# Hedgehog linear attention beside a Mish feed-forward on one core: the kv sum in four column groups, and a new order of all steps

## The chip, the core and the metric

The kernel runs on one core of one Trainium2 chip. Five engines work side by side: TensorE (matmuls; PE in the profile, PEld for its weight loads), VectorE (DVE), ScalarE (ACT), GpSimd (POOL) and SyncE (SP), which here only issues DMA transfers. Each engine runs its own instructions in the order in which the program hands them to it, and semaphores tie the engines together. The metric is the device time of one execution in microseconds, lower is better; the median of several runs is given.

## The reference, cut to what matters

The input x has 2048 tokens of 448 features. It is normalized (LayerNorm without weights), goes through a linear attention of 16 heads of 28 features and, in parallel, through a feed-forward layer with Mish; both are added to x.

```python
xn = layernorm(x)                                    # [2048, 448]
# A: linear attention, H = 16 heads, Dh = 28
q, k, v = split_heads(xn @ wqkv)
pq, pk = einsum("bhsd,hdf->bhsf", q, w_phi), einsum("bhsd,hdf->bhsf", k, w_phi)
phi_q = concat([softmax(pq), softmax(-pq)], -1)      # 56 per head
phi_k = concat([softmax(pk), softmax(-pk)], -1)
kv = einsum("bhsf,bhsd->bhfd", phi_k, v)             # 56 x 28 per head
z  = einsum("bhsf->bhf", phi_k)
num = einsum("bhqf,bhfd->bhqd", phi_q, kv)
den = einsum("bhqf,bhf->bhq", phi_q, z)[..., None] + 1e-6
A = (num / den) merged over heads @ wo
# B: feed-forward, 1792 wide
h = xn @ w1 + b1
B = (h * tanh(softplus(h))) @ w2
out = x + A + B
```

## The kernel before

Tokens are worked on in 16 tiles of 128, taken in 8 pairs `u`. The program is a list of named steps, `ORDER` (L147). `run_order` calls them one after the other, and each call appends its instructions to the engines' streams; `Program.resolve` then puts in the waits that the data need. So `ORDER` alone sets the order on every engine and in every queue, and a step can put instructions on several engines at once. An engine does not pass over an instruction that waits.

The steps, in the names that the order uses (`u` is a pair, `t` a tile; a last letter names the engine: `d` DVE, `a` ACT, `p` POOL, `m` DMA, `s` SP's queue, `b` ACT and DVE with one half each):

- Loads. `lx0` to `lx6`: tiles of x (two tiles each; `lx4` and `lx6` four). `lkm`, `lkt`, `lvm`: the columns of wqkv for k, its last 64 rows for k and v, the columns for v, into `Wkv`. `lqT0` to `lqT3`: the q columns through a transposing DMA into `WqT` (`load_qT`, L285). `l1m0` to `l1m2`, `l1t`: W1. `l2`: the whole of W2 (`load_w2`, L305, one transfer). `lo`: Wo. `lp`, `lb`: w_phi and b1.
- `z16`: 16 matmuls on constants that keep TensorE busy while the first loads arrive.
- `pm`, `pw`, `pp`, `pk`, `pi`, `pv`: constants that POOL writes (masks, zeros, the identity, ones beside v). `pk` makes a second mask, `mask2`, and clears `KVT`.
- `st`, `rs`, `xn`, `xt`: statistics of one tile, reciprocal standard deviation of a pair, the normalized pair `xn`, and its transposed form `xnT`, through a DMA (`m`) or through TensorE. With `xn..p` the product runs on POOL and needs a small DVE instruction, `sh` (L489).
- `wtk`, `wmk`, `wmq`, `qd`: the weights of k and q are multiplied by w_phi (`Wbd`, made by `bd`), so that q and k are never formed. For k, `Wk` is transposed on TensorE and copied to `WT`; for q, `WqT` comes by DMA, and `qd` copies the last rows a second time on DVE (L289) once all four transfers are there.
- `v`, `k`, `q` with `u` and part 1 or 2: matmuls of one pair (8 in part 1, 6 in part 2; 64 rows each, two row halves of the array at a time). Part 2 is followed by the evacuation: v is copied to `v_all`, k and q go through two exponentials on ACT.
- `kn`: normalizes phi(k): a DVE sum and reciprocal, a POOL product (L635). `e`: a transposing DMA of phi(q) of one tile.
- `f0`, `f1`: the first feed-forward product for half of the tokens, then Mish on ACT.
- `kv` with `u` (L641): the sum of phi(k) times v over the pair's tokens. All pairs accumulate in one bank. The weights of a matmul are two heads of `v_all` with two more columns each (a one in each head's part, for z): 60 columns, placed in column group 0 or 64 of the array, so that two run side by side. What is streamed is phi(k) of the same two heads, 112 columns. Of the 60 x 112 products the blocks of one head with itself are wanted.
- `kvz` (L660): two DVE instructions of 60 partitions by 448 add an epsilon to the rows of z (`epsT`, made by `ep`) and multiply by `mask2`, which clears the blocks of one head with the other; then a transposing DMA makes `KVZ` from `KVT`.
- `nd` (L718): numerator and denominator of one tile, 16 matmuls of 56 rows, then seven or so DVE instructions to the quotient. `ot`: its transposed form.
- `G`, `g`, `wo`: the second feed-forward product and the output projection, into one bank per tile. `sto`, `stt`: stores.

PSUM has 8 banks; most matmul steps take two, the one least recently used.

Of the kernel before, what the change touches and what calls it, by code (L numbers as in the profile page):

```python
# [6 lines left out]
ALU = mybir.AluOpType  # L7
# [7 lines left out]
DH = 28  # L15
# [136 lines left out]
k51 xn0p v42a xt6m kn7.0 e2 k52 v52a kn1.1 xt0m kn7.1 kn5.0 v61a lbs q41 v62d kn4.0 k61 q42 e5 e6 l1ts v01d kn2.1 k62  # L152
# [16 lines left out]
def _kernel(es, nc, A_x, A_wqkv, A_w_phi, A_wo, B_w1, B_b1, B_w2, out):  # L169
# [10 lines left out]
    mask2 = sb("mask2", [P, 2, DH], FP32)  # L180
# [163 lines left out]
    def p_pads():  # L344
        for i in (1, 2, 0):
            op("POOL", lambda e, i=i: e.memset(Eq_of(i).rearrange("p i s (h n) -> p (i s h) n", n=64)[:, :, QP:64], 0.0),
               w=[("Eqp", i)] + ([(n, h) for n in ("WT", "WU") for h in range(2)] if i == 0 else []), tag=f"pp{i}")

    def p_mask2():
        op("POOL", lambda e: e.memset(mask2[:], 1.0), w=[("mask2",)], tag="pk0")  # L350
        for r in range(2):
            lo, hi = HALF[r]
            op("POOL", lambda e, lo=lo, hi=hi: e.affine_select(
                out=mask2[lo:hi], in_=mask2[lo:hi], compare_op=ALU.is_ge, fill=0.0, base=0, channel_multiplier=1,
                pattern=[[-(DH + 2), 2], [0, DH]]), r=[("mask2",)], w=[("mask2",)], tag="pk1")
            op("POOL", lambda e, lo=lo, hi=hi: e.affine_select(
                out=mask2[lo:hi], in_=mask2[lo:hi], compare_op=ALU.is_ge, fill=0.0, base=DH + 1, channel_multiplier=-1,
                pattern=[[DH + 2, 2], [0, DH]]), r=[("mask2",)], w=[("mask2",)], tag="pk2")
        op("POOL", lambda e: e.memset(KVT[:, :, :, :, :].rearrange("p g s x f -> p (g s x f)").bitcast(mybir.dt.uint32),
                                      0), r=[("mask2",)], w=[("KVT", 0), ("KVT", 1)], tag="pk3")  # L360

    def eps_rows():
        for i in range(2):
            op("DVE", lambda e, i=i: e.tensor_reduce(epsT[:, i:i + 1], ap_on(ident[:, DH + i:DH + i + 1],
                                                                          [[64, 2], [DH + 2, 2]]), AX.XY, ALU.add),
# [152 lines left out]
    def xT(u, eng):  # L518
# [6 lines left out]
        if eng == "both":  # L525
# [4 lines left out]
                 [("xnT", u)], f"xTe{u}")  # L530
# [110 lines left out]
    def kv_mm(u):  # L641
# [6 lines left out]
        def f(e):  # L648
            for par in range(2):
                for g in range(G):  # L650
                    for r in range(2):
                        ins = e.matmul(bank(kvb)[64 * r:64 * r + NDW, g * 2 * QP:(g + 1) * 2 * QP],  # L652
                                       v_all[:, u, par, 8 * r + 2 * g:8 * r + 2 * g + 2, :],
                                       E_of(u)[:, :, par, (4 * r + g) * QP:(4 * r + g + 1) * QP],
# [5 lines left out]
    def kvz():  # L660
        kvb = kv_bank[0]
        for r in range(2):
            lo, hi = 64 * r, 64 * r + NDW
            op("DVE", lambda e, r=r, lo=lo, hi=hi: e.scalar_tensor_tensor(
                ap_on(KVT[lo:hi, 0, 0, r, 0:1], [[P, 2 * G], [1, QP]]),
                ap_on(bank(kvb)[lo:hi, 0:1], [[QP, 2 * G], [1, QP]]), epsT[lo:hi, 2:3],
                ap_on(mask2[lo:hi, 0, 0:1], [[0, 2 * G], [1, QP]]), ALU.add, ALU.mult),
               r=[pb(kvb), ("mask2",), ("epsT", 2)], w=[("KVT", r)], tag=f"kvz{r}")
# [49 lines left out]
    def nd(t):  # L718
        b = take2(False)

        def f(e):
            for s in range(2):
                for g in range(G):
                    for r in range(2):
                        at = (s * G + g) * NDW
                        ins = e.matmul(bank(b + r)[:, at:at + NDW], EqT[64 * r:64 * r + QP, t, s * G + g, :],  # L726
                                       KVZ[64 * r:64 * r + QP, 2 * g + s, 64 * r:64 * r + NDW], start=True, stop=True)
# [224 lines left out]
    for n, fn in (("pi", p_ident), ("pm", p_mask), ("pw", p_wbd), ("pv", p_ones), ("pk", p_mask2), ("pp", p_pads)):  # L952
        add(n, fn)
# [55 lines left out]
```

## Time and profile before

| | us |
|---|---|
| median of three runs | 154.15 (153.95 to 154.91) |
| the profiled execution's own time | 154.01 |
| its span, first to last instruction | 152.1 |
| TensorE busy in the span | 145.4 |
| VectorE busy | 102.4 |
| ScalarE busy | 74.1 |
| GpSimd busy | 41.4 |

The profile shows one execution. Its page gives busy shares by engine and by forty slices of the span, the chain of work that ended last, and groups of like instructions with their mean duration and the idle time before them. Asked further, the trace gives the instructions of a stretch in order of time, the issues of SP's queue, and the busy time of every engine in chosen stretches. A row of the timeline reads: start, length from the first to the last of the group, engine (SPq is SP's issuing), line, operation, what is written from what, shape, how many, and in brackets the idle time of the engine before it and what ended it. A busy TensorE is not a TensorE at its peak, since a matmul's tail overlaps the next one. Line L438 holds the matmuls of v, k, q and f; L866 those of G and wo.

### The profile page before, as it was taken

Reading aid. Unit: us, or ns where it says so; the run is one execution under the profiler, and the core shown is the slowest. Engines: PE = TensorE matmul, PEld = TensorE weight load, DVE = VectorE, ACT = ScalarE, POOL = GpSimd, SP = SyncE. Lnnn points to the kernel's source line nnn. Section 1 sums busy time; section 2 is a strip of 40 time slices with the busy share of each in tenths; the row PEclk is TensorE's granted clock in tenths of the full one; section 3 lists DMA queues with packets and bytes.
Section 4 is the critical chain, followed back from the end, with each engine's and each line's share of the span. In section 5 each row is a group of like instructions: output and inputs, shape, how many; then the busy total and the mean of one; then the engine's idle time right before and its main releaser. Section 6 shows DMA issues by size and latency. Waiting matters only on the chain.

```text
span 152.1 us, 4002 instructions
## 1 busy us (share of the span) xinstructions
PE 145.4 (96%) x1735; PEld 76.1 (50%) x1735; DVE 102.4 (67%) x224; ACT 74.1 (49%) x96; POOL 41.4 (27%) x59
## 2 busy tenths in 40 slices
PE   7799997999899999999989999999999999999993
PEld 3475543556455584445434445444555555554552
DVE  0997999999999503059998378999373377252452
ACT  3889989796979994776756387100000000000000
POOL 7704743799899970000000000000000000000000
PEclk9999999999999999999999999999999999999999
DMA  5999759989999998840913510803300016003025
GB/s 136 294 136 337 156 166 161 251 158 136 198 190 173 251 271 207 157 89 0 98 37 59 39 26 0 65 2 65 60 0 4 16 49 181 0 4 60 0 100 201
DMA packets 39997, 17.24 MB, mean 113 GB/s; under 512 B 33964, under 2 KB 39212, under 8 KB 39980
## 3 DMA queue, kind: packets, MB, share of 16 engines
q1 hardware_dynamic: 39372, 16.87, 53.5%
q8 instruction: 13, 0.21, 0.6%
q10 hardware_dynamic: 608, 0.12, 0.4%
q14 instruction: 4, 0.03, 0.1%
HBM read 7.02 MB, written 1.84 MB: 58 GB/s over the span
## 4 chain that ended last, share of the span: by engine, by line
PE 69%; DVE 18%; SPq 6%; DMA 3%; ACT 2%; issue 1%
PE PS L438 32%; PE PS L866 28%; DVE stats L467 4%; PE PS L828 3%; SPq L285 3%; DMA x_all<-in_A_x_dram 3%; DVE v_all L745 3%; DVE v_all L747 2%; PE PS L652 2%; PE PS L726 2%; DVE v_all L749 2%; DVE xn L752 2%; DVE v_all L516 1%; DVE mv L468 1%; ACT actT L684 1%
## 5 line engine op out<-in xcount | busy, mean ns | idle before, releaser
L438 PE MATMUL PS<-xnT,W 64*128 64x512 bf16 x392 | 44.9, 376 | 0.9 <-ACT actT L623 0.5
L866 PE MATMUL PS<-W,actT 64*128 64x448 bf16 x392 | 38.7, 349 | 0.0
L703 ACT ACTIVATE actT<-PS,b1T 128x1024 bf16<-128x1024 f32 x28 | 29.8, 1113 | 13.4 <-PE PS L438 13.3
L438 PEld LDWEIGHTS PS<-xnT,W 64*128 64x128 bf16 x392 | 18.9, 94 | 21.7 <-DVE v_all L747 0.9
L866 PEld LDWEIGHTS PS<-W,actT 64*128 64x128 bf16 x392 | 18.8, 94 | 17.2
L635 POOL TENSOR_TENSOR actT<-actT,rSk 128x896 bf16<-128x896 bf16 x16 | 26.6, 1702 | 1.9 <-DVE rSk L633 1.3
L793 DVE TENSOR_TENSOR x_all<-PS,x_all 128x448 bf16<-128x448 f32 (+1 forms) x16 | 9.1, 615 | 15.8 <-PE PS L866 15.1
L631 DVE TENSOR_REDUCE Sk<-actT 128x32 f32<-128x896 bf16 x16 | 16.8, 1047 | 0.2
L741 DVE COPY Sq<-PS 128x16 f32<-128x16 f32 x32 | 4.0, 167 | 17.1 <-PE PS L726 17.0
L623 ACT ACTIVATE actT<-PS 128x896 bf16<-128x896 f32 x16 | 13.7, 923 | 1.0 <-PE PS L438 0.9
L438 PE MATMUL PS<-Wpk,xnT 64*128 64x448 bf16 x112 | 12.9, 350 | 1.0 <-DVE rSk L633 0.8
L438 PE MATMUL PS<-Wkv,xnT 64*128 64x448 bf16 x112 | 12.6, 349 | 0.0
L438 PE MATMUL PS<-Wpq,xnT 64*128 64x448 bf16 x112 | 12.5, 349 | 0.0
L467 DVE BATCH_NORM_STATS2 stats<-x_all 128x6 f32<-128x448 bf16 x14 | 8.5, 607 | 4.3 <-DMA x_all<-in_A_x_dram 4.3
L749 DVE TENSOR_TENSOR v_all<-v_all 128x464 f32<-128x464 f32 x16 | 10.3, 642 | 0.6
L745 DVE TENSOR_TENSOR v_all<-PS,Sq 128x464 f32<-128x464 f32 x16 | 10.3, 641 | 0.5
L752 DVE TENSOR_TENSOR xn<-v_all,rden 128x448 bf16<-128x448 f32 x16 | 10.0, 625 | 0.6
L747 DVE TENSOR_TENSOR v_all<-PS,Sq 128x464 f32<-128x464 f32 x16 | 10.1, 630 | 0.0
L684 ACT ACTIVATE actT<-PS 128x896 bf16<-128x896 f32 x10 | 8.6, 912 | 1.4 <-PE PS L438 1.4
L438 PEld LDWEIGHTS PS<-Wpk,xnT 64*128 64x128 bf16 x112 | 5.5, 94 | 5.8 <-DVE rSk L633 1.2
L438 PEld LDWEIGHTS PS<-Wpq,xnT 64*128 64x128 bf16 x112 | 6.0, 94 | 4.8
L438 PEld LDWEIGHTS PS<-Wkv,xnT 64*128 64x128 bf16 x112 | 5.8, 94 | 4.8 <-issue 0.6
(88 smaller groups left out, 128.8 us busy)
## 6 DMA issues: line engine op xcount, KB each, us to landing
W<-in_B_w_dram SPq DMA_DIRECT2D x1, 1568.0 KB, 7.5
out_dram<-x_all SPq DMA_DIRECT2D x7, 224.0 KB, 2.1
W<-in_B_w_dram SPq DMA_DIRECT2D x3, 448.0 KB, 4.2
x_all<-in_A_x_dram SPq DMA_DIRECT2D x4, 224.0 KB, 3.8
x_all<-in_A_x_dram SPq DMA_DIRECT2D x2, 448.0 KB, 4.2
Wkv<-in_A_wqkv_dram SPq DMA_DIRECT2D x2, 336.0 KB, 4.6
Wo<-in_A_wo_dram SPq DMA_DIRECT2D x2, 336.0 KB, 5.0
W<-in_B_w_dram SPq DMA_DIRECT2D x2, 224.0 KB, 4.8
```

What stands on the lines that cost most here:

```text
L438: ins = e.matmul(o, lhs(c, k), rhs(c, k), start=part == "1" and c == 0, stop=part == "2" and c == 2)
L467: op("DVE", lambda e: e.bn_stats(stats[:, t, :], x_all[:, t, :]), r=[("x", t)], w=[("st", t)], tag=f"bn{t}")
L623: op("ACT", lambda e, s=s: e.activation(E_of(u)[:, s, :, :], two(b, D), ACT.Exp, scale=1.0 if s == 0 else -1.0), r=[pb(b), pb(b + 1)], w=[ ...
L631: op("DVE", lambda e: e.tensor_reduce(Sk[u][:, s, :], Eh(), AX.X, ALU.add), r=[("E", u, s)], w=[("Sk", u, s)], tag=f"Sk{u}.{s}")
L635: op("POOL", lambda e: e.tensor_tensor(Eh(), Eh(), ap_on(rSk[u][:, s, 0:1], [[1, 2 * H], [0, DH]]), ALU.mult), r=[("E", u, s), ("rSk", u, ...
L684: op("ACT", lambda e, s=s: e.activation(Eq_of(u)[:, :, s, :].rearrange("p i (h n) -> p i h n", n=64)[:, :, :, 0:QP], two(b, D).rearrange(" ...
L703: op("ACT", lambda e: e.activation(actT[:, fc, q * 1024:(q + 1) * 1024], bank(b, 2), ACT.Mish, bias=b1T[:, fc:fc + 1]), r=[("b1T",), pb(b) ...
L745: op("DVE", lambda e: e.tensor_tensor(tv(t1[i]), num(0), sx(1), ALU.mult), r=[pb(b), pb(b + 1), ("Sq", i, 1)], w=[("t1", i)], tag=f"ta{t}")
L747: op("DVE", lambda e: e.tensor_tensor(tv(t2), num(1), sx(0), ALU.mult), r=[pb(b), pb(b + 1), ("Sq", i, 0)], w=[("t2",)], tag=f"tb{t}")
L749: op("DVE", lambda e: e.tensor_tensor(t1[i], t1[i], t2, ALU.add), r=[("t1", i), ("t2",)], w=[("t1", i)], tag=f"tc{t}")
L752: op("DVE", lambda e: e.tensor_tensor(o_sb[(t // 2) % 2][:, t % 2, :].rearrange("p (h d) -> p h d", d=DH), t1[i][:, :, 0:DH], ap_on(rden[i ...
L866: ins = e.matmul(bank(places[par][0])[:, 0:D], l, r, start=fresh[par], stop=places[par][2] and i >= len(todo) - 2)
```

## The change

Four things change.

1. The kv sum takes one head a matmul: 30 columns of `v_all` as weights in one of four 32-column groups of the array, 56 columns streamed; 32 matmuls per pair for 16. Only wanted blocks are formed.
2. `mask2` goes. `kvz` becomes four DVE instructions of 30 partitions by 224 elements, one for each column group; POOL only clears `KVT`. `epsT` and the read of `KVZ` in `nd` follow the new spacing of 32.
3. `p_pads` becomes three steps of their own (`pp0`, `pp1`, `pp2`).
4. `ORDER` is new throughout. Among it: `l2s` (W2) stands behind `lvms`; `x1` and `x2` load from ACT's queue; `z10` for `z16`; `b1` is at the start; `wmq0` and `wmq1` stand directly behind `k11`; `wmq0`, one more statistic and other copies change engine.

```diff
 ORDER = """
-pm pw lx3s pp pk lx1s lkms lkts st6d lpa table pi st7a st2d st3d rs3t xn3d lvms rs1a z16 xn1d bd wtk0b wtk1b lx2s xt3b
-pv xt1d wmk0b wmk1a lqT0 st5a st4d lqT2 rs2a v31a lqT1 lqT3 qd lx6s v11a lx4s v32d wmq1a lx0s k11 xn2p st15d st14d st10d
-l1m0s wmq0a st8d rs7p k12 xn7p st1d st9d k31 xt2m q11 l1m1s k32 v12d rs4p st12d xt7m st11d q31 q12 q32 q21 xn4d rs5p
-st13d v21d rs6a q22 xn5d st0d xt4m k21 xt5m v22d v71a k22 v72a rs0p k71 l1m2s k41 kn3.1 e3 k72 k42 xn6d v41a v51a ep e4
...
-q51 v02d e7 q52 kn1.0 k01 b1 e10 k02 q61 kn3.0 f1.21 e9 q62 e11 f1.22 f1.31 f0.21 e12 e8 f1.51 e13 f1.32 f1.52 kn5.1 los
-f0.22 q71 kn2.0 q01 q72 l2s f0.11 f1.01 kn6.1 q02 f1.02 kn6.0 f0.12 kn4.1 kv2 kv3 kv5 kv1 kv4 kn0.0 kn0.1 kv6 kv0 kv7
-f1.131 f1.71 f0.51 kvz f0.81 f1.72 f0.52 f0.82 f1.132 f1.81 f0.131 f1.82 nd3 e15 f1.11 e1 e0 f0.132 f1.12 f1.121 nd2
...
+pw pk lx1a pv pi lba pm lx3s pp2 z10 lkms lpa lkts lvms st3d pp1 table st2a rs1a st7d l2s lx2a st6d rs3t b1 wtk0a xn1d
+xn3d xt1d lx6s bd wtk1b st5d xt3a wmk0a st4d lx4s wmk1a v11d st14d lqT2 v31a pp0 st15d v12a lqT1 lqT3 lqT0 qd lx0s rs2p
+l1m0s v32a xn2p st9d rs7a k11 wmq0d wmq1a xn7p st11d k12 st10d k31 q31 st1d rs5p k32 q11 q32 xt2m st8d xn5d rs4p st13d
+xt7m q12 v21d xn4p q21 xt5m st12d v22d e7 v71d xt4m st0d rs6a q22 rs0p l1m1s v72d k71 k51 k72 xn0p k21 k52 e6 v41d xn6d
...
+f1.51 f0.21 e13 e10 e9 f0.12 f0.22 f1.52 kn0.1 q71 q01 los q72 kn0.0 kn2.0 f0.91 q02 kn6.0 kv2 kv0 kv6 kv7 kn3.0 kv4 kv5
+ep kv1 kv3 f0.71 kvz f0.92 f0.131 f0.81 f0.132 f0.72 f0.31 f0.101 f0.32 nd3 e0 f0.82 e14 f0.102 f0.121 f0.01 f0.122
...
+nd8 wo22 sto1 G22 ot4m wo01 G01 wo61 g14 ot7m wo7F wo41 wob G02 G62 wo7H wo02 G42 wo42 wo62 sto0 sto2 g15 stt14 sto4
+sto6 sto3 stt15
 """
...
-    def p_pads():
-        for i in (1, 2, 0):
+    def p_pads(which):
+        for i in which:
...
-    def p_mask2():
-        op("POOL", lambda e: e.memset(mask2[:], 1.0), w=[("mask2",)], tag="pk0")
-        for r in range(2):
...
+    def p_zero():
         op("POOL", lambda e: e.memset(KVT[:, :, :, :, :].rearrange("p g s x f -> p (g s x f)").bitcast(mybir.dt.uint32),
-                                      0), r=[("mask2",)], w=[("KVT", 0), ("KVT", 1)], tag="pk3")
+                                      0), w=[("KVT0",)], tag="pk3")
...
             for par in range(2):
                 for g in range(G):
-                    for r in range(2):
-                        ins = e.matmul(bank(kvb)[64 * r:64 * r + NDW, g * 2 * QP:(g + 1) * 2 * QP],
-                                       v_all[:, u, par, 8 * r + 2 * g:8 * r + 2 * g + 2, :],
-                                       E_of(u)[:, :, par, (4 * r + g) * QP:(4 * r + g + 1) * QP],
+                    for j in range(4):
+                        h = 8 * (j // 2) + 2 * g + j % 2
+                        ins = e.matmul(bank(kvb)[32 * j:32 * j + DH + 2, g * QP:(g + 1) * QP],
+                                       v_all[:, u, par, h, :], E_of(u)[:, :, par, h * DH:(h + 1) * DH],
                                        start=(first and par == 0 and g == 0), stop=(last and par == 1),
                                        skip_group_check=True)
...
     def kvz():
         kvb = kv_bank[0]
-        for r in range(2):
-            lo, hi = 64 * r, 64 * r + NDW
-            op("DVE", lambda e, r=r, lo=lo, hi=hi: e.scalar_tensor_tensor(
-                ap_on(KVT[lo:hi, 0, 0, r, 0:1], [[P, 2 * G], [1, QP]]),
-                ap_on(bank(kvb)[lo:hi, 0:1], [[QP, 2 * G], [1, QP]]), epsT[lo:hi, 2:3],
-                ap_on(mask2[lo:hi, 0, 0:1], [[0, 2 * G], [1, QP]]), ALU.add, ALU.mult),
-               r=[pb(kvb), ("mask2",), ("epsT", 2)], w=[("KVT", r)], tag=f"kvz{r}")
+        for j in range(4):
+            lo, hi = 32 * j, 32 * j + DH + 2
+            op("DVE", lambda e, j=j, lo=lo, hi=hi: e.tensor_scalar(
+                ap_on(KVT[lo:hi, 0, 0, j // 2, (j % 2) * DH:(j % 2) * DH + 1], [[P, 2 * G], [1, DH]]),
+                ap_on(bank(kvb)[lo:hi, 0:1], [[DH, 2 * G], [1, DH]]), epsT[lo:hi, 2:3], 0.0, op0=ALU.add, op1=ALU.add),
+               r=[pb(kvb), ("KVT0",), ("epsT", 2)], w=[("KVT", j)], tag=f"kvz{j}")
...
                         ins = e.matmul(bank(b + r)[:, at:at + NDW], EqT[64 * r:64 * r + QP, t, s * G + g, :],
-                                       KVZ[64 * r:64 * r + QP, 2 * g + s, 64 * r:64 * r + NDW], start=True, stop=True)
+                                       KVZ[64 * r:64 * r + QP, 2 * g + s, 64 * r:64 * r + 64].rearrange(
+                                           "p (h c) -> p h c", c=32)[:, :, 0:DH + 2], start=True, stop=True)
```

On SP's queue the first issues were x3, x1, Wk, the two tails, Wv, x2, the four of WqT, x6, x4, x0, W1's first chunk; they become x3, Wk, the two tails, Wv, W2, x6, x4, the four of WqT, x0, W1's first chunk. On TensorE the steps after the weights of k were v31, v11, v32, wmq1, k11, wmq0, k12, k31, q11, k32, v12, and become v11, v31, v12, v32, k11, wmq0, wmq1, k12, k31, q31, k32, q11. On DVE `qd` is followed by `sh` of pair 2 (of `xn2p`).

More of the change, by code (lines that the diff above doesn't have):

```diff
@@ L529, in xT @@
             evac("ACT", lambda: xnT[:, u, 0:3, :].rearrange("p c n -> p (c n)"), lambda: bank16(b)[:, 0:3 * P], [pb(b)],
-                 [("xnT", u)], f"xTe{u}")
+                 [("xnT", u)], f"xTh{u}")
             evac("DVE", lambda: xnT[:, u, 3:7, :].rearrange("p c n -> p (c n)"), lambda: bank16(b + 1)[:, 0:4 * P],
@@ L951, in _kernel @@
     add("qd", double_qT)
-    for n, fn in (("pi", p_ident), ("pm", p_mask), ("pw", p_wbd), ("pv", p_ones), ("pk", p_mask2), ("pp", p_pads)):
+    for n, fn in (("pi", p_ident), ("pm", p_mask), ("pw", p_wbd), ("pv", p_ones), ("pk", p_zero)):
         add(n, fn)
+    for i in range(3):
+        add(f"pp{i}", p_pads, (i,))
     for n in (4, 8, 10, 12, 14, 16, 18, 20):
```

23 lines of the change are left out of this document (7 added, 16 removed).

## The prediction

> **What bounds the kernel now.** I read the page first (shares, slices, chain), then the busy time by stretch, then the timelines of TensorE and of SP's queue. The page:
>
> ```profile
> span 152.1 us, 4002 instructions
> PE 145.4 (96%) x1735; PEld 76.1 (50%) x1735; DVE 102.4 (67%) x224; ACT 74.1 (49%) x96; POOL 41.4 (27%) x59
> ...
> DMA  5999759989999998840913510803300016003025
> ...
> PE 69%; DVE 18%; SPq 6%; DMA 3%; ACT 2%; issue 1%
> ```
>
> TensorE is the bound, and the DMA engines are full for most of the first 60 us. By stretches (length, PE busy, PEld, DVE, ACT, POOL, granted clock, DMA share, GB/s):
>
> ```profile
> 18.00:31.00 13.00, 12.01 (x126) 6.30 (x124) 12.62 (x30) 11.34 (x16) 7.38 (x12) 1.00 0.89 183
> 31.00:54.00 23.00, 22.52 (x225) 12.21 (x221) 19.84 (x31) 20.62 (x24) 22.48 (x14) 1.00 1.00 182
> ...
> 70.00:100.00 30.00, 28.93 (x400) 13.68 (x396) 25.00 (x60) 16.17 (x15) 0.00 (x0) 1.00 0.38 41
> 100.00:149.10 49.10, 49.10 (x559) 25.55 (x556) 26.66 (x59) 0.00 (x0) 0.00 (x0) 1.00 0.18 46
> ...
> 12.00:16.00 4.00, 4.00 (x49) 2.16 (x48) 3.31 (x9) 3.82 (x10) 2.30 (x5) 1.00 0.97 362
> ...
> 2.00:8.00 6.00, 5.17 (x35) 2.67 (x34) 4.19 (x12) 3.97 (x14) 4.28 (x16) 1.00 1.17 283
> ...
> 55.00:58.50 3.50, 3.50 (x112) 2.83 (x108) 1.02 (x2) 3.47 (x4) 1.18 (x3) 1.00 1.09 356
> ```
>
> From 18 us on TensorE idles 1.0 us up to 31, 0.5 up to 54 and 1.1 between 70 and 100: 2.6 us is all that any order can win there. Its instructions run in the order written, so a stall near the start is paid at the end, less what of this idle time it swallows.
>
> **The change, part by part.** *Loads.* W2, whole, moves in SP's order from behind the Wo loads to behind Wv, ahead of x6, x4, the four transposing loads of WqT, x0 and W1. x1 and x2 move to ACT's queue. SP's issues now (start, length), the size and issue-to-landing time of each kind, and the spread for transfers into WqT (later ones, from xn, among them):
>
> ```profile
> 3.43 0.59 SPq L273 DMA_DIRECT2D Wkv<-in_A_wqkv_dram  x1
> 4.06 0.49 SPq L270 DMA_DIRECT2D x_all<-in_A_x_dram  x1
> 4.59 5.11 SPq L285 DMA_TRANSPOSE WqT<-in_A_wqkv_dram  x4
> 9.74 1.54 SPq L270 DMA_DIRECT2D x_all<-in_A_x_dram  x3
> ...
> W<-in_B_w_dram SPq DMA_DIRECT2D x1, 1568.0 KB, 7.5
> x_all<-in_A_x_dram SPq DMA_DIRECT2D x4, 224.0 KB, 3.8
> x_all<-in_A_x_dram SPq DMA_DIRECT2D x2, 448.0 KB, 4.2
> Wkv<-in_A_wqkv_dram SPq DMA_DIRECT2D x2, 336.0 KB, 4.6
> ...
> DMA to landing us min/median/max: 2.9/3.2/4.6
> ```
>
> A transposing load alone lands 2.9 us after its issue; one with Wv and x2 in front of it took 4.6. So the queue works in its order, and what stands in front is paid. Wv was issued at 3.43 and takes 4.6: it lands at 8.0, now and after, since the bytes in front of it are the same. Behind it come, after the change: W2, 1568 KB at the 356 GB/s of stretch 55.00:58.50, which was nearly all W2 (4.5 us); x2's 224 KB, sharing the DMA engines from ACT's queue (0.6); x6 and x4, 896 KB at the 362 GB/s of 12.00:16.00 (2.5); WqT, 4 x 112 KB of transposes at the 182 GB/s of 31.00:54.00, where the engines were full of such work (2.5). WqT is whole at 8.0 + 4.5 + 0.6 + 2.5 + 2.5 = 18.1. Bounds: 14 if the queue did not hold it back, 19.3 with W2 at the 283 GB/s of 2.00:8.00. W2 is read first by the G steps, in the second half, so its early arrival wins nothing; in its old place, behind Wo, it stands in front of the transpose of KVT alone, which is covered (below).
>
> *Who waits.* Today:
>
> ```profile
> 11.37 0.23 DVE L289 COPY WqT<-WqT 128x256 bf16<-128x256 bf16 x1 [0.33 <-DMA WqT<-in_A_wqkv_dram]
> 11.77 0.57 PE L585 MATMUL PS<-Wbd,WqT 112*128 112x112 bf16 x8
> 12.27 0.93 PE L438 MATMUL PS<-Wpk,xnT 64*128 64x448 bf16 x8
> 13.13 0.57 PE L585 MATMUL PS<-Wbd,WqT 112*128 112x112 bf16 x8
> 13.63 1.50 PE L438 MATMUL PS<-Wpk,xnT 64*128 64x448 bf16 x14
> 14.97 0.92 PE L438 MATMUL PS<-Wpq,xnT 64*128 64x448 bf16 x8
> 15.72 0.73 PE L438 MATMUL PS<-Wpk,xnT 64*128 64x448 bf16 x6
> 16.29 0.73 PE L438 MATMUL PS<-Wkv,xnT 64*128 64x448 bf16 x6
> 16.86 2.81 PE L438 MATMUL PS<-Wpq,xnT 64*128 64x448 bf16 x28
> ```
>
> DVE's copy (qd) waits for WqT and starts the products of WqT (wmq) 0.4 us after the landing. In the new order wmq0 stands behind k11, and everything else of TensorE behind wmq0; on DVE, qd holds sh2 (so xn2 on POOL, xt2's transfer and v21) and most of the statistics.
>
> *When TensorE gets there.* ACT's first part is now longer, by these rows:
>
> ```profile
> L514 ACT ACTIVATE v_all<-PS 128x896 bf16<-128x896 f32 x3 | 2.8, 931 | 0.1
> L463 ACT ACTIVATE junk<-x_all,rmean 128x448 bf16<-128x448 bf16 x2 | 1.3, 668 | 0.1
> L480 ACT ACTIVATE lnv<-mv,eps_col 128x1 f32<-128x1 f32 x2 | 0.6, 280 | 0.0
> ...
> 0.84 4.96 PE L376 MATMUL PS<-const-bfloat16-1.0 128*128 128x512 bf16 x16 [0.84 <-PEq L994]
> 6.51 1.39 PE L561 MATMUL PS<-ident,Wkv 128*112 128x128 bf16 x16 [0.72 <-DMA Wkv<-in_A_wqkv_dram]
> ```
>
> x1 is there near 4.5 (issued at 0.8; its kind takes 3.8); st2a (some 1.8 in five pieces) ends at 6.3, rs1a at 6.8, the issue of x2 at 7.2, rs3t (four pieces) at 8.1. Then ACT alone empties wtk0 (1.0), half of wtk1 (0.6), xt3, wmk0, wmk1 (0.93 each): Wpk is done at 12.5. TensorE follows it: wmk1 ends near 10.5, then v11, v31, v12, v32, 28 matmuls at 94 ns (2.6; the 28 at 16.86 take 2.81 with the tail of the last), to 13.1; k11 (8 of them) to 13.9. There wmq0 waits until 18.1 + 0.4 = 18.5: a stall of 4.6 us. Fewer warm-up matmuls (10 for 16) cost nothing: TensorE waits for Wkv until 6.5 today, too.
>
> *The lag.* At 18.5 today's kernel has done what the new one has, and besides: wmq0 and wmq1 (1.1), 20 matmuls of k12, k31 and k32, the 8 of q11, and some 17 of the 28 of q that start at 16.86: 45 at 94 ns, 4.3. Lag 5.4 us.
>
> *What is won back.* Behind the stall, v21 waits for xt2: sh2 at 18.6, xn2 1.7 on POOL, transfer 3.4, so 23.7; wmq, k1, k3, q1, q3 fill 5.6 us up to 24. The next tiles follow by the same step, so I count the 1.0 us of idle time before 31 as swallowed, and half a microsecond of the later 1.6.
>
> *The kv sum.* 128 matmuls of 60 columns by 112 become 256 of 30 by 56, in four groups. (First two lines: chain; start, length. Last: busy, mean ns, idle before.)
>
> ```profile
> 54.16 3.27 PE PS L652 x128
> ...
> 65.95 0.22 PE PS L726 x16
> ...
> L664 DVE SCALAR_TENSOR_TENSOR KVT<-PS,epsT,mask 60x448 bf16<-60x448 f32 x2 | 1.4, 683 | 5.9 <-PE PS L652 5.9
> ```
>
> Now 25.5 ns from start to start. The streamed columns per group halve, so 1.6 us if four groups run as well as two (a gain of 1.7); 6.5 if each start still takes 25.5 (a loss of 3.3). The weight columns are the same 7,680 in all, and the nearest row with matmuls as short (nd, 16 in 0.22) has 13.8 ns a start: 256 x 13.8 = 3.5. I take +0.2. [...]
>
> *Small parts.* kvz: four instructions of 30x224 for two of 60x448; at half the length each between 0.34 and 0.5, so 0 to +0.6 on DVE; nine f parts stand between kv3 and nd3, 64 matmuls, over 6 us at 94 ns, and cover up to 2.0 of kvz and some 3.4 of the transpose behind it. If that cover were gone, +0.6. Five POOL instructions of the second mask go, early, with nobody waiting. nd reads KVZ with a gap after 30 columns: the same count of columns, which excludes a gain; 0, up to +3.5 if the gap doubled its 0.22 a tile (16 tiles). Exchanges of engines (one statistic more and wmq0 on DVE, half-evacuations and xn4 off it; xn4 and rs2 on POOL) leave DVE's sum before kv within 0.5 us; POOL gains 1.7 us, ahead of its first kn. Moves of f, G, wo and nd leave TensorE's work as it is: 0, between -1.1 (the idle time in 70 to 100) and +1.1 (as much again).
>
> *Sum* against the profiled execution, 154.01 us with a span of 152.1 (1.9 around it; 0.14 under the median of the runs): +5.4 - 1.0 - 0.5 + 0.2 = +4.1, so 158.1; I say 158.0.
>
> **The rivals.**
> *Faster: W2 passes beside the rest.* If WqT lands before 14 us, TensorE does not stop. It is then 1.4 us behind at 13.9 (wmq0, wmq1 and 0.3 of k12), wins 1.0 and 0.5 of idle time and, with four groups at full rate, 1.6: 152.3. For it: the direct loads reach 362 GB/s while the first ones moved more slowly. Against: 4.6 against 2.9 us for a transfer behind others, and 1568 KB more in front.
> *Nothing in sum.* The stall is half as long (WqT at 16) and kv takes its best value: +5.4 - 2.2 - 1.5 - 1.6, 154.1. For it: the queue is fed without the pauses it has today (5.11 us for four transposing issues).
> *Half clock behind the stall.* The first warm-up weight loads start 0.42 us apart, the last eight take 1.63 together:
>
> ```profile
> 1.65 0.15 PEld L376 LDWEIGHTS PS<-const-bfloat16-1.0 128*128 128x128 bf16 x1 [0.28 <-issue]
> 2.07 0.15 PEld L376 LDWEIGHTS PS<-const-bfloat16-1.0 128*128 128x128 bf16 x1 [0.28 <-issue]
> ...
> 3.67 1.63 PEld L376 LDWEIGHTS PS<-const-bfloat16-1.0 128*128 128x128 bf16 x8 [0.16 <-issue]
> ```
>
> After idleness the array ran at half rate for 2.8 us, although the granted clock reads 1.00. If 4.6 us of stall bring that back, 1.4 us more: 159.5. [...]
> *Each start of kv at 25.5 ns.* The forecast and 3.1 more: 161.1. For it the present gap; against it nd's.
>
> **How the numbers follow.** Forecast 0.50; half clock 0.13; 25.5 ns a start 0.05; nothing in sum 0.12; faster 0.20. The time is the first one's, 158.0, its own range 155.8 to 159.5. The range 153.0 to 160.5 leaves out most of the faster case and the 161.1. A measurement tells about 1% here (1.5 us). Slower by more: 0.68 (the first three); within: 0.13 (nothing in sum); faster by more: 0.19.
>
> **What would show it.** In the new profile DVE's copy to WqT starts near 18 and waits for its DMA, and PE shows one gap of 4 to 5 us before L585 on WqT. W2's landing would be near 12.5. kv shows its 256 matmuls in 3.3 to 3.5 us; the matmuls right behind the gap tell of the clock. If the copy starts before 14, the argument fails at the queue; if the gap is there and the end is not later, it fails at the lag being carried to the end.

## The result, and the profile after

The changed kernel takes 161.9 us (median of four runs, 161.39 to 162.84) where the kernel before takes 154.05 (153.53 to 154.91) beside it: a ratio of 1.051, 95% interval 1.044 to 1.058, so 7.9 us slower. The forecast was 158.0 with a range up to 160.5. The profiled execution took 161.39 us, 7.4 more than that of before. In the changed kernel and most of the variants TensorE's array falls to half clock for some microseconds (3.4 and 6.8 in the profiled execution of the change, at a granted clock of 0.50), at places and for totals that differ between executions; the executions of one kernel spread over 1.2 to 6.7 us, the ratios below leave out those over 1.5% above the fastest of their kernel, and the profiled executions of experiments 2 and 8 are among those left out.

The page of the changed kernel, as shown of before (span, busy shares, clock in forty slices, instruction queue, chain):

```profile
span 159.4 us, 4235 instructions
PE 145.7 (91%) x1857; PEld 77.5 (49%) x1857; DVE 105.9 (66%) x225; ACT 73.4 (46%) x89; POOL 42.2 (26%) x57
...
PEclk9969759999999999999999999999999999999999
...
q8 instruction: 14, 0.23, 0.6%
...
PE 78%; SPq 9%; DMA 7%; issue 3%; DVE 1%; ACT 1%
```

TensorE is busy nearly as long as before (145.7 us for 145.4), so all but 0.3 of the 7.3 us that the span grew are idle time. The waits of TensorE, longest first (line, what ended the wait, total, times, longest):

```profile
PE PS L575 <- DVE WqT L288: 4.5, 1, 4.5
PE PS L643 <- issue: 2.3, 1, 2.3
PE PS L428 <- DMA W<-in_B_w_dram: 1.2, 1, 1.2
PE PS L499 <- DVE xn L491: 1.1, 1, 1.1
PE PS L551 <- DMA Wkv<-in_A_wqkv_dram: 1.0, 1, 1.0
```

The first is the stall that was forecast, at wmq0. The second stands inside the kv sum, and nothing that the profile shows was waited for ("issue"). The chain that ended last, in order of time (start, length), passes through both (L288 is qd, L575 wmq, L643 kv):

```profile
3.58 0.49 SPq L304
4.11 3.49 SPq L269
...
12.50 6.60 DMA WqT<-in_A_wqkv_dram
19.13 0.24 DVE WqT L288
19.41 1.68 PE PS L575 x16
...
64.77 2.32 issue
```

Read it from the top: W2 is issued (L304), then SP's own next instruction, the issue of x6 (L269), takes 3.49 us; the last transposing load of WqT is issued only at 12.50 and needs 6.60 more. Then qd, then wmq0. The issues of SP's queue up to 16 us, with size and median time to landing:

```profile
W<-in_B_w_dram SPq DMA_DIRECT2D x1, 1568.0 KB, 10.1
x_all<-in_A_x_dram SPq DMA_DIRECT2D x2, 448.0 KB, 9.5
...
Wkv<-in_A_wqkv_dram SPq DMA_DIRECT2D x1, 336.0 KB, 5.4
...
WqT<-in_A_wqkv_dram SPq DMA_TRANSPOSE x4, 7.4
```

W2 lands at 3.58 + 10.1 = 13.7, behind Wv (2.95 + 5.4 = 8.35); x6 and x4, which stand behind it, need 9.5 where such transfers took 4.2. The timeline of TensorE around the stall and in the kv sum, and the busy time of the stretch behind it, after and then before (length; PE, PEld, DVE, ACT, POOL; granted clock; DMA share; GB/s):

```profile
19.41 1.68 PE L575 MATMUL PS<-Wbd,WqT 112*128 112x112 bf16 x16 [4.46 <-DVE WqT L288]
21.02 2.79 PE L428 MATMUL PS<-Wpk,xnT 64*128 64x448 bf16 x14
...
62.74 2.04 PE L643 MATMUL PS<-actT,v_all 128*30 128x56 bf16 x227
67.10 0.38 PE L643 MATMUL PS<-actT,v_all 128*30 128x56 bf16 x29 [2.32 <-issue]
```

```profile
17.50:24.50 7.00, 5.09 (x36) 2.90 (x38) 4.93 (x15) 2.70 (x4) 4.39 (x8) 0.51 0.45 129
62.70:67.40 4.70, 2.38 (x258) 2.19 (x256) 0.50 (x1) 4.40 (x5) 0.80 (x3) 1.00 0.02 5
70.00:100.00 30.00, 30.00 (x394) 14.52 (x392) 20.87 (x52) 20.03 (x20) 0.00 (x0) 1.00 0.40 68
```

```profile
17.50:24.50 7.00, 6.85 (x74) 3.38 (x72) 6.83 (x19) 6.27 (x10) 3.54 (x9) 1.00 0.67 155
```

The 14 matmuls of k12 and k31 behind the stall take 2.79 us; the same 14 took 1.50 before. The granted clock is 0.51 in that stretch. From the start of wmq0 to that of v21 (19.41 to 27.26) pass 7.85 us; the same steps in the same order take 5.44 in experiment 12 below, at full clock (14.61 to 20.05): 2.4 us lost on top of the stall. That TensorE's busy time grew by no more than 0.3 us is a balance: on one side this 2.4, on the other 1.1 fewer for warm-up (3.87 for 4.96) and 0.9 fewer for the matmuls of kv; smaller parts on both sides were not added up. Further on, between 70 and 100 us, TensorE no longer idles at all (1.07 before): the late idle time was swallowed, as expected. The kv sum has 2.38 us of work in 4.7 us of time.

### The profile page after: what moved, and what is told of

Its sections match the earlier page's. It is cut to its first block, busy times and chain, and to the rows that moved or that the text cites. A ratio compares the mean times of both kernels' runs of the same rounds, so it can differ in the third digit from the quotient of the medians.

```text
span 159.4 us, 4235 instructions
## 1 busy us (share of the span) xinstructions
PE 145.7 (91%) x1857; PEld 77.5 (49%) x1857; DVE 105.9 (66%) x225; ACT 73.4 (46%) x89; POOL 42.2 (26%) x57
## 4 chain that ended last, share of the span: by engine, by line
PE 78%; SPq 9%; DMA 7%; issue 3%; DVE 1%; ACT 1%
PE PS L428 40%; PE PS L856 29%; DMA WqT<-in_A_wqkv_dram 4%; PE PS L818 3%; DMA W<-in_B_w_dram 3%; SPq L269 3%; SPq L284 3%; PE PS L715 2%; PE PS L643 1%; SPq L280 1%; PE PS L575 1%; SPq L681 1%; SPq L511 1%; PE PS L834 1%; SPq L272 1%
## 5 line engine op out<-in xcount | busy, mean ns | idle before, releaser
L457 DVE BATCH_NORM_STATS2 stats<-x_all 128x6 f32<-128x448 bf16 x15 | 9.1, 609 | 7.7 <-DMA x_all<-in_A_x_dram 7.7
L428 PE MATMUL PS<-Wpk,xnT 64*128 64x448 bf16 x112 | 13.8, 377 | 0.0
L737 DVE TENSOR_TENSOR v_all<-PS,Sq 128x464 f32<-128x464 f32 x16 | 10.1, 629 | 0.0
L486 POOL TENSOR_SCALAR xn<-x_all,rstd,shift 128x448 bf16<-128x448 bf16 (+2 forms) x12 | 7.0, 596 | 7.8 <-DVE shift L479 5.5
L428 PEld LDWEIGHTS PS<-Wpk,xnT 64*128 64x128 bf16 x112 | 6.0, 99 | 5.5 <-issue 1.3
## 6 DMA issues: line engine op xcount, KB each, us to landing
W<-in_B_w_dram SPq DMA_DIRECT2D x1, 1568.0 KB, 10.1
```

The lines of the kernel that those rows point to most:

```text
L428: ins = e.matmul(o, lhs(c, k), rhs(c, k), start=part == "1" and c == 0, stop=part == "2" and c == 2)
L457: op("DVE", lambda e: e.bn_stats(stats[:, t, :], x_all[:, t, :]), r=[("x", t)], w=[("st", t)], tag=f"bn{t}")
L737: op("DVE", lambda e: e.tensor_tensor(tv(t2), num(1), sx(0), ALU.mult), r=[pb(b), pb(b + 1), ("Sq", i, 0)], w=[("t2",)], tag=f"tb{t}")
```

## Experiments

Most change one thing, in the old or the new order. A token of `ORDER` is a step, so a moved load is one token. All ratios are to the kernel before on the same chip; "+5.2 us" is ratio less one, times 154. Differences between two rows of the table are differences of such values.

| kernel | ratio, 95% | us to before |
|---|---|---|
| the change | 1.051 (1.044 to 1.058) | +7.9 |
| 1: old order, W2 early | 1.034 (1.030 to 1.038) | +5.2 |
| 2: the change, W2 late | 1.026 (1.018 to 1.034) | +4.0 |
| 3: the change, W2 behind WqT | 1.027 (1.018 to 1.035) | +4.1 |
| 4: old order, new kv | 1.032 (1.028 to 1.036) | +4.9 |
| 5: the change, old kv | 1.017 (1.010 to 1.024) | +2.6 |
| 6: the change, kv spread out | 1.076 (1.070 to 1.082) | +11.7 |
| 7: old order, new kv spread out | 1.018 (1.012 to 1.023) | +2.7 |
| 8: the change, matmuls in the stall | 1.045 (1.038 to 1.053) | +7.0 |
| 9: the change, 16 warm-up matmuls | 1.043 (1.039 to 1.047) | +6.6 |
| 10: the change, W2 late and old kv | 1.002 (0.998 to 1.006) | +0.3 |
| 11: 10, and other loads back | 0.995 (0.991 to 0.998) | -0.8 |
| 12: 11, and 16 warm-up matmuls | 0.994 (0.992 to 0.997) | -0.9 |

### The place of W2

**1. The old kernel with W2 moved to where the change has it.**

```diff
-... xn3d lvms rs1a z16 ...  q01 q72 l2s f0.11 ...
+... xn3d lvms l2s rs1a z16 ...  q01 q72 f0.11 ...
```

> The kernel before with that one load moved the other way: W2 directly behind Wv. Theory: WqT lands near 16.5 us in place of 11.35, TensorE gets a gap of 4 to 5 us before the first product of WqT, the clock behind it is halved for a while, and the time rises by 5 to 7 us, to 159 to 161. Rival (W2's place does not matter by itself, the new order does): within 1 us of the kernel before, 154.

Measured: +5.2 us. TensorE's timeline shows the gap alone, before its L585 on WqT, and half the pace behind it (the 8 of k11 took 0.93 before); below it the stretch behind the gap:

```profile
15.88 0.64 PE L585 MATMUL PS<-Wbd,WqT 112*128 112x112 bf16 x8 [3.67 <-DVE WqT L289]
16.45 1.68 PE L438 MATMUL PS<-Wpk,xnT 64*128 64x448 bf16 x8
```

```profile
16.20:19.70 3.50, 3.50 (x28) 1.56 (x26) 3.13 (x9) 1.60 (x4) 2.54 (x5) 0.51 0.95 367
```

One moved token is enough for two thirds of the loss: a stall of 3.67 us (4 to 5 were expected), and 3.5 us at clock 0.51 behind it.

**2. The change with W2 back behind q72.**

```diff
-... st7d l2s lx2a st6d ...  q72 kn0.0 ...
+... st7d lx2a st6d ...  q72 l2s kn0.0 ...
```

> The changed kernel with one load moved: W2 goes back behind the loads of Wo. Theory (W2 in front of x6, x4 and WqT in SP's queue makes the stall at wmq0): WqT is whole near 13.9 us in place of 19.1, TensorE's 4.5 us gap before the product of WqT shrinks to under 0.6, the granted clock stays at 1.00 behind it (2.0 us), and the time falls by 6 to 7 us, to 155 (154 to 156.5). Rival (the place of wmq0 right behind k11, or the other moved steps, make it): the gap stays above 3 us and the time above 160.

Measured: +4.0 us, 3.9 better than the change, but short of what was expected: in the profiled execution a gap of 2.34 us at wmq0 stayed, and half clock behind it (its stretch stands in the last section). DVE's timeline shows why; qd does not wait for WqT any more:

```profile
13.12 0.63 DVE L457 BATCH_NORM_STATS2 stats<-x_all 128x6 f32<-128x448 bf16 x1 [3.24 <-DMA x_all<-in_A_x_dram]
...
16.14 0.23 DVE L288 COPY WqT<-WqT 128x256 bf16<-128x256 bf16 x1
```

DVE waits 3.24 us for x2, which now loads from ACT's queue, then works off four statistics that the new order has in front of qd, then copies at once. In the new order the place of qd on DVE, and x2's late landing, are a second cause that W2 had covered; in experiments 3 and 10 qd starts as late, at 16.07 and 15.96. The kv pause was 2.97 us in this run.

**3. The change with W2 directly behind the loads of WqT.** x6 and x4 stay in front of them.

```diff
-... st7d l2s lx2a st6d ...  lqT3 lqT0 qd ...
+... st7d lx2a st6d ...  lqT3 lqT0 l2s qd ...
```

> The changed kernel with W2 moved back by six places only, directly behind the four loads of WqT: as early as can be without standing in front of them. Theory (the queue's order makes the gap, not the bytes moved in the first 20 us): WqT lands near 13.7 us as with W2 at its old place, the gap at wmq0 is 2 to 2.6 us (x2 lands at 13 and stands in front of DVE's copy), and the time is that of the kernel with W2 wholly back, 157 to 160. Rival (the bytes themselves slow the first loads, wherever W2 stands): WqT lands after 16.5 us and the gap stays above 3.5.

Measured: +4.1 us, as with W2 wholly back, though not by the expected gap of 2 to 2.6 us at wmq0. TensorE's waits in this kernel have none for WqT; apart from the kv pause the longest is:

```profile
PE PS L428 <- DMA xnT<-xn: 1.9, 1, 1.9
```

qd ran at 16.07 for 19.13. So what counts is what stands in front of WqT in SP's queue. That W2's bytes slow everything, wherever they are, would have left the copy at 19. What is behind W2 now pays instead: xt2's transposing transfer, 1.9 us. In the profiled run the array was at clock 0.50 from 8.6 to 15.4 us, so that TensorE came late to wmq0 (16.88); that wmq0 had no gap says nothing by itself, the start of qd does.

### The kv sum

**4. The old order with the new kv, kvz and nd.**

```diff
-            for r in range(2):                       # 60 columns by 112
+            for j in range(4):                       # 30 columns by 56
```

> The order of the kernel before with the new kv sum, kvz and mask alone. Theory A (TensorE runs out of fetched instructions in the dense run of 256 short matmuls): two stretches of matmuls of 2.0 to 2.4 us together with one pause of 2 to 2.7 us in them that ends with nothing the profile names; the kv sum takes 4.3 to 5.1 us from first to last where it took 3.27, and the time is 1 to 1.6 us longer, 155.0 to 155.7. Theory B (the pause seen in the changed kernel is a wait for pair 3's data, which come last there): no pause above 0.5 us here, kv in 2.1 to 2.4 us, time 153.0 to 153.3.

Measured: +4.9 us, several times what was expected (1 to 1.6). TensorE's timeline of kv, and the stretch behind it:

```profile
54.13 1.75 PE L643 MATMUL PS<-actT,v_all 128*30 128x56 bf16 x192
56.08 0.45 PE L643 MATMUL PS<-actT,v_all 128*30 128x56 bf16 x36 [0.20 <-POOL actT L625]
60.04 0.36 PE L643 MATMUL PS<-actT,v_all 128*30 128x56 bf16 x28 [3.52 <-issue]
60.34 9.85 PE L428 MATMUL PS<-xnT,W 64*128 64x512 bf16 x74
```

```profile
60.40:63.80 3.40, 3.40 (x21) 1.23 (x20) 1.79 (x4) 0.00 (x0) 0.00 (x0) 0.50 0.18 50
```

The matmuls themselves take 2.56 us, less than the 3.27 of before. But 3.52 us of pause stand in front of the last 28, no engine or transfer is named as its end, and behind it the array runs at clock 0.50 for 3.4 us: the 74 matmuls there take 9.85 us, and at the 111 ns each of the next experiment's (58 in 6.43) they would take 8.2, 1.6 less.

**5. The change with the old kv, kvz and nd.** W2 is still early.

```diff
-            for j in range(4):                       # 30 columns by 56
+            for r in range(2):                       # 60 columns by 112
```

> The new order with the old kv sum (128 matmuls in two column groups, old kvz and mask). Theory (the dense run of 256 short matmuls makes TensorE run out of instructions): the pause of 2.3 us in the kv sum goes, the sum takes 3.3 us in one piece (2.35 in two pieces and the pause before), and the time falls by 1 to 2 us against the changed kernel's 161.9; the gap at wmq0 stays at 4.5. Rival (the new kv sum gains its 0.9 us and the pause comes from the order): the pause stays and the time rises by 0.5 to 1 us.

Measured: +2.6 us, 5.3 better than the change, where 1 to 2 were expected. The stall at wmq0 is there in full and kv has no pause:

```profile
19.20 1.68 PE L585 MATMUL PS<-Wbd,WqT 112*128 112x112 bf16 x16 [4.96 <-DVE WqT L289]
...
60.65 3.34 PE L652 MATMUL PS<-actT,v_all 128*60 128x112 bf16 x128
63.92 6.43 PE L438 MATMUL PS<-xnT,W 64*128 64x512 bf16 x58
```

Not all of the 5.3 is the kv sum's own. Of the 3.5 us between the two profiled executions (157.9 and 161.39) kv takes 1.4; the other 2.1 are there when kv starts (60.65 for 62.74): v21 came 0.8 earlier, and the change's wait of 1.16 us for W1 is missing. Half clock differs from execution to execution, too: a stretch of 3.4 us of it lowers the mean granted clock of an execution by 0.011; the four of the change have 0.957 to 0.968, three or four such stretches, and those here 0.978 or 1.00, two or none.

**Where the pause stands.** Experiments 8 and 9, told below, add matmuls ahead of kv: 20, and 6 (16 warm-up matmuls for 10). Their timelines of kv:

```profile
62.40 1.86 PE L643 MATMUL PS<-actT,v_all 128*30 128x56 bf16 x206
66.69 0.63 PE L643 MATMUL PS<-actT,v_all 128*30 128x56 bf16 x50 [2.42 <-issue]
```

```profile
61.15 1.99 PE L643 MATMUL PS<-actT,v_all 128*30 128x56 bf16 x221
65.31 0.44 PE L643 MATMUL PS<-actT,v_all 128*30 128x56 bf16 x35 [2.17 <-issue]
```

The change pauses after 227 matmuls of kv, these after 206 and 221: 21 and 6 earlier. So the pause belongs to a place in TensorE's stream of instructions, counted from the program's start, and not to a pair of tokens, a piece of data or a moment: in all eight kernels with the new kv it stands behind 727 or 728 matmuls. POOL, which writes phi(k), is no cause either. In the change its products (start, length) ended at 39.95 + 23.24 = 63.2 us, 1.6 before the pause began:

```profile
39.95 23.24 POOL L625 TENSOR_TENSOR actT<-actT,rSk 128x896 bf16<-128x896 bf16 x14
```

What fits is the supply of instructions. The queue for them moved 14 packets in the kernels with the new kv (0.23 MB, 16 KB each) and 13 with the old one (0.21 MB), where the change has 122 more matmuls with their weight loads (1857 for 1735), 244 instructions. The 227 matmuls with their weight loads are 454 instructions in 2.04 us, 4.5 ns each; the old kv has 256 in 3.3 us, 13 ns each. No view names the refill as what TensorE waits for, so this is inferred; but the trace of the change holds the start and length of every packet of that queue. One packet runs from 64.49 to 65.72 us, across the start of the pause, and the DMA engines do hardly anything else there (columns as above, the last GB/s; 12 GB/s in 1.40 us are some 16 KB):

```profile
64.40:65.80 1.40, 0.37 (x45) 0.27 (x32) 0.00 (x0) 1.40 (x2) 0.00 (x0) 1.00 0.06 12
65.80:67.10 1.30, 0.00 (x1) 0.00 (x1) 0.00 (x0) 1.28 (x2) 0.00 (x0) 1.00 0.00 0
```

TensorE goes on at 67.10, 1.38 us behind the packet's end and 2.61 behind its start. In experiment 4, with the longest pause (3.52), the DMA engines were full throughout it (357 GB/s from 56.50 to 60.05, W2 issued at 54.11); that this is what makes it longer is not shown, nor is what passes between a packet's end and the next matmul.

**6. The change with three feed-forward steps between pairs of kv.**

```diff
-... kv2 kv0 kv6 kv7 kn3.0 kv4 kv5 ep kv1 kv3 f0.71 kvz f0.92 f0.131 f0.81 ...
+... kv2 kv0 f0.71 kv6 kv7 f0.92 kn3.0 kv4 kv5 f0.131 ep kv1 kv3 kvz f0.81 ...
```

> The changed kernel with three steps of the first feed-forward product moved up between the pairs of the kv sum (after pairs 0, 7 and 5), nothing else. Theory A (instructions run out): with slower matmuls between them the pause of 2.3 us goes (none above 0.6), and the time falls by 1.7 to 2.4 us to 159.5 to 160.2. Theory B (pair 3's data): a pause before pair 3 stays, less at most the 2.1 us of the three moved steps that now stand ahead of it, and the end of kv stays where it is: 161.5 to 162.

Measured: +11.7 us, and the time tells nothing of the pause. The moved f0.92 writes its Mish where phi(k) of pair 3 lies, which in this kernel is overwritten before it is summed; DVE's sum over phi(k) of that pair waits 10.8 us for the Mish, and the last pair of kv waits 2.34 us. The pause itself stands where the count puts it, behind 205 matmuls of kv and the 22 moved ones, and lasts 0.58 us, as theory A has it; but the new waits stretched the sum, too.

**7. The old order with the new kv, six feed-forward steps between its pairs.**

```diff
-... kv2 kv3 kv5 kv1 kv4 kn0.0 kn0.1 kv6 kv0 kv7 ...
+... kv2 f0.31 kv3 f0.32 kv5 f0.01 kv1 f0.02 kv4 f0.51 kn0.0 kn0.1 kv6 f0.52 kv0 kv7 ...
```

> The order of the kernel before with the new kv sum, and six steps of the first feed-forward product (f0.3, f0.0, f0.5, 42 matmuls) moved in between its pairs. Theory (the pause comes from consuming over 240 instructions faster than the next block of them can be fetched, some 3.5 us): stretched to 6.6 us the sum has no pause above 0.8 us, no half clock follows, and the time is 153 to 154.5, where the same sum in one piece took 158.4 to 161. Rival (the short matmuls in four column groups cost by themselves): above 157.

Measured: +2.7 us (median 157.63), not the 153 to 154.5 of the theory. TensorE's timeline at the place of the pause:

```profile
62.24 0.39 PE L643 MATMUL PS<-actT,v_all 128*30 128x56 bf16 x32
63.47 0.82 PE L428 MATMUL PS<-xnT,W 64*128 64x512 bf16 x6 [0.84 <-issue]
```

The pause shrinks from 3.52 to 0.84 us, and the clock stays at 1.00: spreading the dense part out does what the supply theory says. The time is still above before. In the profiled execution kv starts 1.1 us later than before (55.30 for 54.16), after waits for xnT and W1 that no moved step makes; in the sum the first moved step waits 0.79 us for ACT, and the pause takes 0.84. The rest was not traced, so that the short matmuls cost something by themselves, as the rival had it, is not excluded. A kernel that keeps the gain of four groups was not found.

### The clock

**8. The change with 20 matmuls on constants in front of wmq0**, to keep the array busy through the stall.

```diff
-... rs7a k11 wmq0d wmq1a ...
+... rs7a k11 z20 wmq0d wmq1a ...
```

> The changed kernel with 20 matmuls on constants put in front of wmq0, where TensorE waits 4.5 us for WqT (20 at 0.21 us fill 4.3 of it); nothing they compute is used. Theory (the array runs at half rate for some 5 us behind that gap, for its idleness): the granted clock between 17.6 and 24.5 us rises from 0.51 to 1.00, the 36 matmuls there take 3.2 in place of 5.2 us, and the time falls by 1.5 to 2.2 us, to about 160. Rival (behind the gap the tiles' transfers set the pace, not the array): the clock may rise, but the next matmuls wait as long for xnT and the time stays within 0.7 us of the changed kernel's 161.9.

Measured: +7.0 us, 0.9 under the change with overlapping intervals (expected: 1.5 to 2.2). Busy time behind the stall, and behind the kv pause:

```profile
17.60:24.50 6.90, 6.90 (x65) 3.77 (x65) 4.50 (x14) 3.10 (x5) 3.92 (x8) 1.00 0.37 106
66.90:70.30 3.40, 3.40 (x61) 1.41 (x46) 1.79 (x4) 0.00 (x0) 0.00 (x0) 0.51 0.02 5
```

The first stretch rose from clock 0.51 to 1.00, and from wmq0 to v21 (20.25 to 25.68) pass 5.43 us instead of 7.85. Since the added matmuls hold wmq0 for 0.84 us, v21 is 1.6 us earlier than in the change. Then, in this run, the half clock came behind the kv pause and took it back. That the idle array is the cause of the low clock is shown by the first row; the time saved in the end is not, though the one of its four executions with a mean clock of 1.00 took 160.46 us, near the 160 expected.

**9. The change with 16 warm-up matmuls for 10.**

```diff
-pw pk lx1a pv pi lba pm lx3s pp2 z10 ...
+pw pk lx1a pv pi lba pm lx3s pp2 z16 ...
```

> The changed kernel with 16 warm-up matmuls for 10 and nothing else. Theory (in the changed kernel the early half clock is hidden, since TensorE waits for WqT until 19 us anyway): the gap at wmq0 grows from 4.5 to 5 to 6.5 us, WqT lands at 19.1 as before, and the time stays within 1 us of 161.9. Rival (the early half clock is part of the loss): the time falls by 1.5 to 3 us.

Measured: +6.6 us, 1.3 under the change, between theory and rival; the intervals just overlap. Between 7.4 and 10.8 us the granted clock is 1.00 in this kernel and 0.50 in the change. The stall covers most of that: its length is 4.55 us, and wmq0 starts at 19.03 instead of 19.41. Half clock behind the stall is shorter here, 3.4 us for 6.8, and v21 starts 1.2 us earlier (26.09 for 27.26).

### Both undone

**10. The change with W2 late and the old kv.** The rest of the new order stays.

```diff
-... st7d l2s lx2a st6d ...  q72 kn0.0 ...
+... st7d lx2a st6d ...  q72 l2s kn0.0 ...
-            for j in range(4):                       # 30 columns by 56
+            for r in range(2):                       # 60 columns by 112
```

> The new order with W2 back behind Wo and with the old kv sum. Theory (these two make the loss, the rest of the order is about neutral): only the gap of 2 to 2.5 us at wmq0 is left, with one stretch of 3.4 us at half clock behind it (x2 lands at 13 us on ACT's queue, and DVE's copy of WqT stands behind the statistics of x2 and x6); 153 to 155 us, within 1 us of the kernel before. Rival (the rest of the order costs, too): 156 or more.

Measured: +0.3 us, no change that can be told (ten runs). With both parts undone the loss is gone. The expected gap at wmq0 does not show in the profiled run: half clock, from 7.1 to 14.0 us, let TensorE come there only at 16.40, after qd (15.96).

**11. The same with the other loads back:** x2 and WqT on SP's queue ahead of x6 and x4, qd ahead of the statistics of x6.

```diff
-... lvms st3d ...  st7d lx2a st6d ...  v11d st14d lqT2 v31a pp0 st15d v12a lqT1 lqT3 lqT0 qd ...
+... lvms lx2s lqT2 lqT1 lqT3 lqT0 st3d ...  st7d st6d ...  v11d qd st14d v31a pp0 st15d v12a ...
```

> The new order with the old kv sum, W2 back behind Wo, x2 and the four of WqT back in front of x6 and x4 on SP's queue, and DVE's copy of WqT ahead of the statistics of x6; still 10 warm-up matmuls. Theory (what the loads and the kv sum cost is then gone; what is left is the idle time that the new order saves late, and half clock early): WqT lands near 11.5 us, no gap at wmq0 above 0.5 us, a stretch of half clock before 14 us stays, and the time is 151.5 to 153.5. Rival (the rest of the new order is no better than the old one): 154 to 155.

Measured: -0.8 us (median 153.31), the interval just below 1 (0.991 to 0.998). As expected, qd (11.22) no longer holds wmq0 (13.89, no gap). The half clock early is not in the profiled run; eight of the ten have a mean clock of 0.989 or less.

**12. The same with 16 warm-up matmuls.**

```diff
-pw pk lx1a pv pi lba pm lx3s pp2 z10 ...
+pw pk lx1a pv pi lba pm lx3s pp2 z16 ...
```

> The same with 16 warm-up matmuls for 10. Theory (the six matmuls that the change took away let TensorE idle from 4.7 us on, and the array fell to half rate for 3.4 to 6.8 us of the first 14; that is not free once nothing else waits there): the granted clock is 1.00 up to 20 us in the profile, and the time falls by 1 to 2 us against the run with 10, to 150.5 to 152, below the kernel before by 1 to 2 per cent. Rival (the first loads set the pace there): the same time as with 10, within 0.5 us.

Measured: 152.93 us (152.49 to 153.67, eight runs) for 153.73: ratio 0.994 (0.992 to 0.997). The gain of 1 to 2 us against the run with 10 did not come: the two are the same, as the rival had it. It beats both kernels, by 0.9 us (0.6%) and, by the two ratios, by 8.8, and its runs lie closer together than those of 11 (151.62 to 155.35), with a granted clock of 0.999 or more in all. Its TensorE goes through wmq0 without a gap:

```profile
14.61 0.96 PE L585 MATMUL PS<-Wbd,WqT 112*128 112x112 bf16 x16
```

## Why the prediction was right in its direction and too low

**Right: the queue works in its order.** The step that carried the forecast put WqT at 18.1 us and the stall at 4.6; DVE's copy started at 19.13, the stall is 4.46. Experiments 1 to 3 show that the place of W2 in front of WqT is the cause. The term was 1.0 us short: Wv landed 0.35 later, and W2 took 13.7 - 8.35 = 5.3 us for 4.5 (its 1568 KB at 300 GB/s, between the two rates of the bounds); what stood behind W2 took 5.4 for 5.6. SP was itself held for 3.49 us at the next issue, which the sum did not have, but the last load of WqT was issued (12.50) before W2 had landed, so no time is shown to be lost by it. TensorE came later, too (14.95 for 13.9), which is why the stall is not longer.

**Right: the lag is carried to the end, less the later idle time.** The 1.07 us between 70 and 100 were swallowed. Against it stands a new wait of 1.16 us for the last part of W1, which the sum did not have.

**Wrong: the kv term, +0.2.** The busy time was within its bounds and better than the value taken: 2.04 + 0.38, less the tail, for the 3.5 assumed; 227 matmuls in 2.04 us are 9.0 ns a start, below the 13.8 ns of the nd row. But from the first to the end kv takes 4.7 us (62.74 to 67.48) for 3.27, +1.4, because of a pause of 2.32 that is in no bound and no rival. The step that failed is the one that took the kv sum's time from its busy time: the bounds asked how fast the array can start matmuls, and not how fast instructions arrive. Alone, in the old order, the new kv costs 4.9 us, since the pause there is 3.52 and half clock follows.

**Wrong: full clock behind the stall was taken as likeliest.** Half clock was a rival at 0.13 with a price of 1.4. It came, and cost 2.4 us in the profiled run; and it came in experiments 1, 2, 5 and 9, too, behind gaps of 3.67, 2.34, 4.96 and 4.55 us. That idleness brings it held (clock 0.51 behind the stall, 1.00 with the stall filled, experiment 8); the chance and the size were the error. The size: half clock lasted from 17.66 to 24.49 us, and 5.1 us of that lie behind the stall, where 2.8 were priced. The chance of 0.13 was the author's estimate, and no run shows what it rests on; in the change and in these four experiments half clock stood behind the stall each time.

**Wrong in its reason: "fewer warm-up matmuls cost nothing".** The argument was that TensorE waits for Wkv anyway. The clock was not asked: with 10 the array is at half clock from 7.4 to 10.8 us, with 16 it is not (experiment 9). Here the stall hides most of the cost. Without the stall the two differ in the spread of the times (151.62 to 155.35 against 152.49 to 153.67) more than in the median (experiments 11 and 12).

**Right: kvz is covered.** Four instructions instead of two, within the bounds of 0.34 and 0.5 each, as the row of its tile shows, and nd3 waits for nothing:

```profile
L654 DVE TENSOR_SCALAR KVT<-PS,epsT x4: 440/446/460, 67.6 to 69.0; 30x224 bf16<-30x224 f32 x4
```

**The sum again, with these sizes:** 158.1, plus 1.0 (WqT), 1.2 (kv, +1.4 for +0.2) and 2.4 (clock) is 162.7 against 161.4 in the profiled execution, and the wait for W1 would make it 163.9. Some of the 2.5 too many is the late idle time, of which 1.07 us were swallowed where half a microsecond was counted; the rest is in terms that overlap and were not taken apart. What closes is TensorE's own account. Four of its waits before are gone after:

```profile
PE PS L438 <- DVE rSk L633: 0.8, 1, 0.8
PE PS L726 <- DVE v_all L747: 0.6, 2, 0.4
PE PS L438 <- ACT actT L623: 0.5, 1, 0.5
PE PS L438 <- DVE v_all L747: 0.5, 1, 0.5
```

With a fifth of 0.2 that is 2.6 us. New are the stall (4.5), the pause (2.3), the wait for W1 (1.2), one for xn (1.1) and 0.5 of small ones, 9.6 us. The difference of 7.0 and 0.3 more of busy time are the 7.3 us of the span. Of the rivals, "W2 passes beside the rest" and "nothing in sum" needed WqT by 14 to 16 us; neither came near. 25.5 ns a start for kv was far off.

## What to carry to other kernels

Price a moved load by what stands behind it in its queue and by the first reader of that, not by when its own data are read: one token cost 5.2 us in experiment 1. Before cutting matmuls into more and smaller ones, count instructions against time; behind 454 TensorE instructions in 2.04 us came a pause, and it (2.3 us) cost more than the smaller matmuls saved (0.9). The gaps of 2.34 to 4.96 us on TensorE in front of wmq0 were paid twice here, once as a gap and once at half clock behind it, so filling matmuls at the start are worth judging by the clock and not by the wait they stand in.

## What was not expected of the hardware

- A fixed place in the instruction stream cost 2.2 to 3.5 us when 454 TensorE instructions had been run in 2.04 us, and 0.84 us when the same matmuls were spread over 10 us; in the change it ended 1.38 us behind a packet of 16 KB on the queue of instructions.
- Half clock came behind gaps of 2.34 us (experiment 2, the stretch below) and of 2.42 (experiment 8), though not behind the pause of 2.32 in the change. In the trace of the change the granted clock changes at 7.42, 10.84, 17.66 and 24.49 us, at whole multiples of 3.41 us from one another. Cut into such windows, the two at full clock with the most time without a matmul have half clock behind them (1.90 us from 4.01 on, 2.71 from 14.25 on), and the third does not (1.65 from 65.45 on). The pause lies across 65.45, which cuts it into 0.68 and 1.65 us; so where a gap lies may count, but one trace does not show it.

```profile
16.90:20.30 3.40, 3.40 (x26) 1.70 (x25) 3.30 (x10) 2.25 (x4) 3.24 (x7) 0.51 0.24 47
```

- With Wv and W2 (1,904 KB) ahead in its queue, SP itself was held 3.49 us at the issue of x6, a plain load of 448 KB; before, the issues of three loads of x took 1.54 us together.
